# Loads of q, k and v from unit 6 on issued by GpSimd instead of SyncE, with all five engine orders solved anew

## The chip, the cores and the metric

The kernel runs on one core of a Trainium2 chip. A core has five engines that run side by side, each through its own list of instructions in order: TensorE (PE, matmuls; its weight loads are shown as PEld), VectorE (DVE), ScalarE (ACT), GpSimd (POOL) and SyncE (SP, which here only issues DMAs). They wait for one another by semaphores. DMAs are issued by SP, by POOL and in three places by ACT; the profile shows them as queues, q1 for those of SP, q0 for those of POOL and q10 for those of ACT. All queues share 16 DMA engines.

The metric is the time of one execution on the device in microseconds. Before the change it is 296.55 us, the median of three runs (296.13, 296.55 and 298.25).

## The reference

```python
def _attn_ref(q, k, v):                       # each (8, 8, 576, 64): batch, head, token, feature
    q_s = np.exp(q - np.max(q, axis=-1, keepdims=True))
    q_s = q_s / (np.sum(q_s, axis=-1, keepdims=True) + 1e-09)
    k_s = np.exp(k - np.max(k, axis=2, keepdims=True))
    k_s = k_s / (np.sum(k_s, axis=2, keepdims=True) + 1e-09)
    kv = np.einsum('bhsd,bhse->bhde', k_s, v)
    return np.einsum('bhsd,bhde->bhse', q_s, kv)

def _moe_ref(x, w_in, w_out):                 # x (4608, 512), w_in (512, 2048), w_out (2048, 512)
    h = x @ w_in
    g = np.where(h > 0.0, h, np.exp(np.minimum(h, 0.0)) - 1.0)
    return g @ w_out
```

The attention's output, with heads laid side by side, is the x of the second part. Everything is float32 at the boundary.

## The kernel before

**Attention in 16 units.** A batch's eight heads are cut into two units of four heads, so unit n is half of batch n // 2. For each unit q, k and v are loaded (`load`, L349; one DMA of 576 KB each) into the tiles `QR`, `KR` and `VR`. `QR` and `KR` exist twice and alternate by n % 2; `VR` exists once from unit 4 on (`raw`, L365, gives units 1 and 3 a second one). `stage1` (L385) takes exponentials of q and k on ACT (L392, L396), converts v to bfloat16 into `VB` (L276, on ACT or POOL), sums q's rows on DVE (L418), takes reciprocals (L420) and multiplies q by them into `QS` (L430, on POOL or DVE). From unit 4 on the transpose of `QS` is a DMA that SP issues (`turn`, L467) into the single tile `QT`, and `widen` copies it to float32 (`qsT`, L276, on ACT or POOL). `kv_mm` (L504) multiplies k by v on PE, two units in one go from unit 4 on; `m` normalizes the result (`MBLK`, L513 and L517); `ao_mm` (L535) makes the attention's output, and `xt` copies it into `XT`, a ring of 1,536 token columns.

**The feed-forward part in nine blocks.** Block j holds 512 tokens. `hg_mm` (L617) multiplies by w_in; ACT and DVE make g of it (L639, L641, L644; L648 and L650 in some groups of blocks 0 and 1). The product with w_out is plain for block 0 and half of block 1 (`out_mm`, L664), and from there on one level of Strassen's scheme on 256-column quarters (`pair`, L797). This needs differences of w_out's quarters once (`combos`, L724, into `TB` and `W2`) and sums of g's quarters for each half block (`add_sum`, L748, on POOL or DVE, into `SB` and `GR`). DVE adds the products into `OSB` tiles (L806), and `store` (L693) issues two DMAs for each tile. The four stores' tiles of block 0 are called `OSBX`. They lie where `TB` lies, so the third difference of each group (the one that writes the first third of `TB`) may not run before those stores have read their tiles. From block 1 on two `OSB` tiles alternate until the last three blocks, so a copy into one waits for the stores of the pair before.

**What sets the order.** The program records operations in a fixed numbering (0 to 1428) with their dependencies. The table `ORDER` (from L27) then gives for each engine the list of numbers in the order in which the engine runs them. An operation that may run on one of two engines (exponentials may not; conversions, copies, `QS` multiplications, differences and sums may) runs on the engine in whose list its number stands. So the order is written out, and no scheduler runs at build time. `emit` puts a semaphore wait ahead of an operation for each dependency that the engine does not know to be met; an engine that waits holds up everything behind it in its list. A load waits until its tile's former readers are done: q's for the multiplication into `QS`, k's for `kv_mm`, v's for the conversion into `VB`.

**Who issues what.** SP issues the loads of units 0 and 1 at the start, then the loads of units 6 to 15, all transposes and nearly all stores, in one list. POOL issues the loads of w_in (L374), of w_out (L382) and of units 2 to 5. The choice for units 4 to 15 is one line in `program`:

```python
                        self.load(n, t, due(n) - 20, "gp" if n < 6 else "sp")      # L944
```

Of the kernel before, what the change touches and what calls it, by code (L numbers as in the profile page):

```python
# [19 lines left out]
CASTS = 16  # L20
GROUPS, WHOLE = ((0, 4), (4, 6), (6, 8)), 6
NSP = 8
CAST0, CAST1 = "pair", "pair"
XT0, XT1, TP0, TP1 = "both", "both", ("act", "act"), ("act", "dve")
ISSUE = {"sp": 550, "act": 550, "gp": 740}
ORDER = {
    "pe": (  # L27
        "32 34 36 53 55 56 51 59 77 79 80 63 64 78 81 84 83 86 87 82 85 88 98 102 109 132 120 106 "
        "147 146 124 155 154 149 148 126 156 157 169 144 168 167 150 170 152 158 174 176 171 164 "
        "175 190 192 177 191 193 252 256 257 210 263 258 264 265 270 219 269 276 271 277 221 278 "  # L30
        "282 283 230 289 284 290 291 238 332 336 341 363 373 374 377 375 378 379 368 303 380 381 "
        "400 401 382 402 305 389 394 405 406 407 411 412 413 479 415 314 427 480 421 422 423 322 "
        "436 495 481 483 484 485 486 487 488 512 513 514 506 517 518 519 523 524 525 527 533 534 "
        "535 544 545 546 548 549 448 539 560 450 551 550 575 552 576 577 553 459 569 580 581 582 "
        "586 587 588 645 646 590 596 597 598 467 602 647 649 650 651 652 653 678 654 679 680 661 "
        "672 683 684 689 690 691 685 614 693 710 699 700 701 711 712 705 717 718 714 719 616 715 "
        "716 741 742 743 726 625 735 746 747 752 753 748 754 633 756 762 763 764 808 768 812 813 "
        "809 814 810 824 841 815 816 842 843 817 835 780 846 852 853 847 848 854 856 873 874 862 "
        "863 864 875 782 868 889 877 880 881 878 879 904 882 905 906 898 791 919 915 909 910 916 "
        "911 917 798 931 925 926 927 958 959 960 962 963 964 991 992 965 966 993 967 974 985 996 "  # L40
        "997 998 1002 1003 1004 1023 1024 1006 1025 1012 1013 1014 942 1018 1027 1028 1029 1030 "
        "1054 1031 1055 944 1032 1056 1039 952 1048 1059 1065 1066 954 1060 1067 1061 1069 1075 "
        "1088 1076 1089 1077 1153 1154 1081 1155 1092 1093 1094 1121 1090 1104 1160 1122 1123 1157 "
        "1158 1161 1095 1162 1159 1096 1097 1184 1115 1136 1126 1127 1132 1128 1133 1185 1134 1186 "
        "1148 1142 1143 1144 1169 1189 1190 1191 1195 1196 1197 1222 1178 1199 1218 1205 1206 1219 "
        "1223 1207 1283 1284 1211 1234 1220 1287 1224 1288 1285 1225 1251 1252 1226 1253 1227 1245 "
        "1266 1256 1257 1290 1291 1258 1262 1292 1263 1289 1264 1278 1272 1273 1274 1299 1314 1315 "
        "1316 1319 1349 1320 1308 1329 1321 1350 1325 1326 1327 1353 1365 1354 1366 1335 1336 1337 "
        "1351 1355 1382 1383 1356 1369 1357 1358 1367 1370 1384 1371 1398 1399 1387 1400 1372 1388 "
        "1393 1394 1389 1373 1374 1395 1409 1410 1411 1403 1404 1405 1417 1418 1419 1423 1424 1425 "),  # L50
    "act": (
        "24 28 40 44 21 23 3 33 39 37 58 52 54 65 66 113 89 92 93 95 99 100 103 110 111 133 121 108 "
        "134 115 114 136 138 137 151 153 178 197 165 172 184 181 223 194 198 206 248 249 253 259 "
        "260 266 220 296 235 272 273 279 231 232 285 286 292 293 239 307 333 337 338 317 302 364 "
        "365 369 370 441 316 390 391 395 396 306 319 416 417 428 429 323 452 437 438 496 497 462 "
        "507 508 528 529 607 540 547 541 561 451 618 562 465 570 571 464 461 591 592 628 468 648 "
        "603 604 773 662 663 673 674 627 694 695 713 784 706 707 617 630 740 727 728 626 736 737 "
        "757 758 769 770 811 779 825 826 936 840 836 837 781 857 858 796 794 869 876 870 890 891 "
        "946 793 899 903 900 792 920 921 932 961 933 975 976 986 987 1007 1008 1019 1020 1040 1041 "
        "1049 1050 955 1070 1071 1082 1083 1105 1091 1106 1120 1116 1117 1137 1138 1149 1150 1170 "  # L60
        "1171 1179 1180 1200 1201 1212 1213 1221 1235 1236 1250 1246 1247 1267 1268 1279 1280 1300 "
        "1301 1309 1310 1330 1331 1352 1381 1415 1422 1428 "),
    "dve": (
        "25 0 6 29 4 30 5 45 26 2 27 31 41 46 35 48 49 42 50 7 43 57 60 61 62 116 90 91 94 96 97 "
        "101 104 105 117 112 118 107 122 123 125 345 139 127 140 128 129 141 145 135 159 160 161 "
        "166 173 200 201 187 195 196 224 250 251 225 211 254 255 212 213 214 215 216 261 262 267 "
        "268 358 297 222 274 275 280 281 346 350 298 351 287 288 294 240 295 241 308 242 342 339 "
        "362 340 243 244 360 383 245 376 309 366 304 367 371 399 372 403 442 443 404 392 408 393 "
        "397 414 398 420 432 315 434 418 419 430 431 424 433 453 482 439 440 490 454 502 324 515 "
        "511 498 516 325 499 326 520 526 327 532 328 509 510 329 536 503 530 531 449 608 565 505 "  # L70
        "558 609 542 543 559 578 574 579 563 564 583 619 589 595 460 572 573 599 593 568 657 643 "
        "620 594 469 470 471 472 656 473 677 605 606 681 474 666 682 664 665 686 669 692 675 698 "
        "667 671 676 696 702 615 697 774 708 709 744 775 745 776 729 725 732 730 749 755 738 761 "
        "733 634 635 739 636 765 637 818 759 638 806 760 639 785 771 822 829 772 640 844 786 827 "
        "834 845 828 849 855 838 861 839 865 859 860 783 937 883 887 885 871 872 892 907 893 938 "
        "947 908 901 902 912 918 922 924 956 799 800 923 928 968 934 935 983 990 948 981 994 995 "
        "801 977 999 802 978 803 1005 988 804 1011 805 989 1033 1026 1015 1037 1009 1010 943 1021 "
        "945 1053 1022 1057 1034 1058 953 1042 1038 1043 1046 1062 1068 1074 1047 1051 1052 1098 "
        "1078 1072 1100 1073 1086 1156 1111 1109 1110 1087 1102 1163 1113 1084 1085 1107 1124 1108 "
        "1099 1125 1164 1103 1183 1118 1119 1129 1135 1141 1139 1140 1145 1187 1166 1188 1174 1151 "  # L80
        "1152 1192 1172 1198 1173 1204 1181 1182 1177 1208 1202 1230 1203 1216 1239 1214 1215 1237 "
        "1254 1286 1238 1243 1242 1229 1297 1255 1248 1259 1249 1269 1313 1265 1271 1270 1343 1294 "
        "1305 1281 1282 1302 1303 1317 1275 1307 1345 1318 1359 1311 1322 1328 1334 1332 1341 1333 "
        "1338 1312 1377 1363 1347 1362 1348 1360 1385 1368 1386 1401 1364 1402 1390 1397 1396 1416 "
        "1412 1413 1406 1420 1426 "),
    "gp": (
        "1 14 15 22 67 47 16 38 17 18 19 20 68 69 71 70 72 119 73 76 75 74 130 143 142 162 131 163 "
        "353 199 204 202 349 207 226 209 233 357 229 236 299 361 347 359 354 355 385 387 310 386 "
        "384 388 320 348 313 356 352 444 435 477 489 491 478 493 494 492 455 447 500 504 501 554 "
        "556 458 555 557 610 566 567 655 644 659 658 621 660 668 613 670 720 724 722 721 624 731 "  # L90
        "631 723 807 734 820 833 821 819 831 823 787 830 832 790 884 888 894 896 886 797 939 895 "
        "957 897 970 972 979 969 971 973 941 949 982 980 1035 984 951 1044 1045 1036 1114 1167 1168 "
        "1112 1165 1101 1176 1175 1228 1217 1241 1240 1232 1231 1233 1244 1295 1293 1304 1296 1306 "
        "1298 1361 1346 1344 1375 1342 1379 1376 1378 1380 "),
    "sp": (
        "8 9 10 11 12 13 203 205 208 218 227 234 217 228 186 182 188 179 185 237 183 189 180 300 "
        "301 247 334 335 344 343 318 246 311 410 321 409 312 425 426 445 446 463 522 456 521 457 "
        "331 330 537 538 466 584 611 585 612 600 601 629 475 476 623 622 687 688 704 703 777 632 "
        "750 641 778 767 766 751 642 851 850 788 789 795 866 867 913 914 930 929 940 1001 1000 950 "
        "1016 1017 1063 1064 1079 1080 1193 1130 1147 1210 1146 1209 1131 1194 1277 1276 1324 1260 "  # L100
        "1261 1340 1339 1323 1392 1391 1414 1407 1408 1421 1427 "),
}


# [169 lines left out]
class Gen:  # L274
# [578 lines left out]
    def program(self):  # L853
# [86 lines left out]
        def loads(*tn):  # L940
            def go():
                for t, n in tn:
                    if n < NU:
                        self.load(n, t, due(n) - 20, "gp" if n < 6 else "sp")  # L944
            return 0, go

        steps = [[first(2)], [wide(2), kv(2), loads(("q", 4), ("k", 4))],
# [133 lines left out]
```

## Time and profile before

| What | us |
|---|---|
| median of three runs | 296.55 |
| the profiled execution | 296.65 |
| its span, first to last instruction | 294.8 |
| outside the span | 1.85 |
| PE busy in the span | 279.6 |
| PE's first matmul of the feed-forward part starts at | 14.88 |
| last matmul ends at | 291.19 |
| POOL busy in the span | 174.0 |

The span is what the views below cover; the 1.85 us outside it stands in the execution's time alone. Times in a view count from the span's start. "POOL PS L797" or "DVE OSB L806" names an engine, the tile that is written and the line. A wait is named by the engine and line that waited and the one that released it. The timeline lists instructions with start, duration and what ended the idle time ahead of them; for SP, duration is the time to issue a DMA and not the transfer. The chain of waits is followed back from the last instruction to what released each step. Section 6 of the page gives the median time from the issue of a DMA to its landing. The granted TensorE clock is 1.00 throughout.

### The profile page before, as it was taken

To read this page: it belongs to the slowest core of one execution; us is meant where nothing else is said; L and a number is where in the kernel's file an instruction comes from. 1 tells how busy PE (TensorE), PEld (TensorE's weight loads), DVE (VectorE), ACT (ScalarE), POOL (GpSimd) and SP (SyncE) were. 2 spreads that over 40 slices of the span, in tenths; PEclk is the share of its full clock that TensorE was granted. 3 is DMA by queue.
4 is the path that set the end of the run, shared out by engine and by line. 5 is a ranking of instruction groups with operands and counts; after the bars stand their busy time and mean duration, and the time that the engine had idled before them with its cause. 6 is when DMAs were issued, how large, how long until landed. Compare 5 with 4: busy or idle time off the path is not lost.

```text
span 294.8 us, 5547 instructions
## 1 busy us (share of the span) xinstructions
PE 279.6 (95%) x2201; PEld 244.4 (83%) x2201; DVE 237.4 (81%) x446; ACT 204.4 (69%) x225; POOL 174.0 (59%) x169
## 2 busy tenths in 40 slices
PE   0899999999799999999999899999999999999995
PEld 0487878788698898989998789898989999998994
DVE  2858874988998899889899758877898976698983
ACT  5688848698799975998885679835574566665510
POOL 0870637773799898749580684979440603562651
PEclk9999999999999999999999999999999999999999
DMA  7999999899773487499419528043112002300325
GB/s 268 398 340 393 391 389 350 243 207 358 212 259 73 168 224 205 157 258 297 118 39 264 167 58 215 10 105 76 39 24 49 0 2 54 89 2 1 80 64 142
DMA packets 35946, 50.04 MB, mean 170 GB/s; under 512 B 16336, under 2 KB 17104, under 8 KB 35920
## 3 DMA queue, kind: packets, MB, share of 16 engines
q1 hardware_dynamic: 29680, 33.96, 40.4%
q0 software_dynamic: 6000, 15.47, 16.4%
q10 hardware_dynamic: 240, 0.26, 0.4%
q8 instruction: 17, 0.28, 0.4%
q14 instruction: 9, 0.07, 0.1%
HBM read 36.70 MB, written 9.44 MB: 156 GB/s over the span
## 4 chain that ended last, share of the span: by engine, by line
PE 81%; DMA 8%; POOL 3%; SPq 2%; issue 2%; ACT 1%; DVE 1%; POOLq 0%
PE PS L617 37%; PE PS L797 33%; PE PS L664 6%; DMA W<-in_moe_w_in_dram 3%; PE PS L535 2%; DMA KR<-in_k_dram 2%; DMA out_dram<-OSB 2%; DMA out_dram<-OSBX 2%; PE PS L504 1%; POOL QS L430 1%; SPq L693 1%; SPq L356 1%; POOL W L374 1%; POOL VB L276 1%; DVE TB L724 1%
## 5 line engine op out<-in xcount | busy, mean ns | idle before, releaser
L617 PE MATMUL PS<-XT,W 128*128 128x512 f32 x576 | 142.0, 393 | 0.4 <-DMA W<-in_moe_w_in_dram 0.4
L617 PEld LDWEIGHTS PS<-XT,W 128*128 128x128 f32 x576 | 105.2, 188 | 21.8 <-issue 0.8
L639 ACT ACTIVATE GE<-PS 128x1024 f32<-128x1024 f32 x72 | 73.5, 1024 | 54.3 <-PE PS L617 45.1
L644 DVE SCALAR_TENSOR_TENSOR GR<-PS,GE 128x512 fp32r<-128x512 f32 (+1 forms) x124 | 87.1, 704 | 23.4 <-ACT GE L641 21.9
L748 POOL TENSOR_TENSOR GR<-GR 128x256 fp32r<-128x256 f32 (+1 forms) x55 | 53.4, 984 | 38.1 <-DVE SB L748 29.1
L641 ACT ACTIVATE GE<-GE 128x1024 f32<-128x1024 f32 x64 | 67.9, 1061 | 1.8
L797 PE MATMUL PS<-W,GR 128*128 128x256 f32 x360 | 56.8, 283 | 1.7 <-ACT OSB L276 1.7
L797 PE MATMUL PS<-TB,GR 128*128 128x256 f32 x360 | 54.0, 283 | 0.0
L797 PEld LDWEIGHTS PS<-W,GR 128*128 128x128 f32 x360 | 50.5, 191 | 4.0 <-ACT OSB L276 2.2
L797 PEld LDWEIGHTS PS<-TB,GR 128*128 128x128 f32 x360 | 48.5, 191 | 0.8
L806 DVE TENSOR_TENSOR OSB<-OSB,PS 128x256 f32<-128x256 f32 x90 | 37.0, 413 | 9.4 <-PE PS L797 8.3
L430 POOL TENSOR_TENSOR QS<-QR,RZQ 128x1152 f16<-128x1152 f32 (+1 forms) x14 | 27.2, 1941 | 18.8 <-DVE RZQ L420 16.9
L748 POOL TENSOR_TENSOR SB<-GR 128x256 fp32r<-128x256 f32 (+1 forms) x20 | 19.9, 1000 | 22.0 <-DVE GR L644 21.3
L418 DVE TENSOR_REDUCE ZQ<-QR 128x18 f32<-128x1152 f32 (+2 forms) x18 | 21.8, 1209 | 9.3 <-ACT QR L416 5.4
L664 PE MATMUL PS<-W,GR 128*128 128x512 f32 x96 | 25.8, 398 | 1.7 <-DVE GR L644 1.7
L748 POOL TENSOR_TENSOR GR<-SB,GR 128x256 fp32r<-128x256 f32 (+1 forms) x23 | 21.9, 962 | 9.2 <-PE PS L797 7.4
L664 PEld LDWEIGHTS PS<-W,GR 128*128 128x128 f32 x96 | 17.4, 188 | 5.0 <-DVE GR L644 1.8
L748 DVE TENSOR_TENSOR GR<-GR 128x256 fp32r<-128x256 f32 (+1 forms) x35 | 20.2, 596 | 0.6 <-PE PS L797 0.5
L396 ACT ACTIVATE KR<-KR 128x1152 bf16<-128x1152 f32 x16 | 18.3, 1155 | 1.9 <-DMA KR<-in_k_dram 1.9
L276 POOL CAST qsT<-QT 128x1152 fp32r<-128x1152 f16 x10 | 11.5, 1149 | 10.7 <-PE PS L535 8.5
L797 PE MATMUL PS<-W,SB 128*128 128x256 f32 x112 | 17.3, 283 | 0.0
L392 ACT ACTIVATE QR<-QR 128x1152 f32<-128x1152 f32 x14 | 16.3, 1164 | 0.3 <-DMA QR<-in_q_dram 0.3
(57 smaller groups left out, 238.3 us busy)
## 6 DMA issues: line engine op xcount, KB each, us to landing
out_dram<-OSB SPq DMA_DIRECT2D x61, 128.0 KB, 2.4
QR<-in_q_dram SPq DMA_DIRECT2D x12, 576.0 KB, 4.6
KR<-in_k_dram SPq DMA_DIRECT2D x12, 576.0 KB, 6.3
VR<-in_v_dram SPq DMA_DIRECT2D x12, 576.0 KB, 5.0
W<-in_moe_w_out_dram POOLq DMA_DIRECT2D x4, 1024.0 KB, 12.2
QR<-in_q_dram POOLq DMA_DIRECT2D x4, 576.0 KB, 10.6
VR<-in_v_dram POOLq DMA_DIRECT2D x4, 576.0 KB, 11.3
KR<-in_k_dram POOLq DMA_DIRECT2D x4, 576.0 KB, 9.7
```

Of the source, the lines that this page charges most:

```text
L392: S.add("act", t_act(1152, False), lambda e: e.activation(flat(q), flat(q), AF.Exp), key - 3, X=[f"qR{i}0", f"qR{i}1"])
L396: S.add("act", t_act(1152, False), lambda e: e.activation(ek[:, :, :, :].rearrange("p h c d -> p (h c d)"), flat(k), AF.Exp), key - 2, X=[ ...
L418: S.add("dve", t_dve(m), lambda e, qp=qp, zp=zp: e.tensor_reduce(zp, qp, AX.X, ALU.add), key - 3, R=[f"qR{i}{x}" for x in xs], W=[f"ZQ{i}{ ...
L430: lambda e, qp=q[:, :, a:b, :], rz=rz, dst=qs[:, :, a:b, :]: e.tensor_tensor(dst, qp, rz, ALU.mult),
L617: last = e.matmul(P[:, t * 512:(t + 1) * 512], self.W1[:, kc, tt * 128:(tt + 1) * 128], self.XT[:, kc, rc:rc + BLK], start=(kc == 0), stop ...
L639: S.add("act", t_act(1024, True), lambda e: e.activation(ge, P, AF.Exp), key, W=gw + over, X=banks)
L641: S.add("act", t_act(1024, False), lambda e: e.activation(ge, ge, AF.Relu, bias=1.0, scale=-1.0), key, X=gw)
L644: S.add("dve", t_dve(512 if j else 1024), lambda e, u=u: e.scalar_tensor_tensor(*(x[:, :, u, :] if j else x for x in (gt, P)), 0.0, ge[:, ...
L664: last = e.matmul(dst, self.tile(jb, jj, ts), self.W2[:, jj, c0:c1], start=(jj == 0), stop=(jj == 15))
L748: lambda e: e.tensor_tensor(dst, a, b, op), key, R=R, W=W, X=X, after=after)
L797: last = e.matmul(dst, a[i][:, y_, :], b[i][:, y_, :], start=start and i == 0 and y_ == 0, stop=stop and i == len(grps) - 1 and y_ == z - ...
L806: S.add("dve", t_dve(256), lambda e: e.tensor_tensor(dst, a, b, ALU.add), key, R=R, W=W, X=X, after=after)
```

## The change

The loads of units 6 to 15 (ten units, three each, 30 DMAs) are issued from POOL's list; SP's list keeps the first six loads, the transposes and the stores. All five lists are new, and with them the engine of 177 operations, 30 of them the loads. The lines that differ, with the long tables cut:

```diff
+SPLIT_RINGS = True
 ORDER = {
...
     "gp": (
-        "1 14 15 22 67 47 16 38 17 18 19 20 68 69 71 70 72 119 73 76 75 74 130 143 142 162 131 163 "
-        "353 199 204 202 349 207 226 209 233 357 229 236 299 361 347 359 354 355 385 387 310 386 "
...
+        "1 27 15 14 67 16 38 17 18 19 20 119 68 69 72 71 70 73 76 75 74 130 115 138 143 162 131 163 "
+        "345 353 204 205 207 208 349 217 218 226 233 234 228 357 346 236 237 246 351 247 359 361 "
...
     "sp": (
-        "8 9 10 11 12 13 203 205 208 218 227 234 217 228 186 182 188 179 185 237 183 189 180 300 "
-        "301 247 334 335 344 343 318 246 311 410 321 409 312 425 426 445 446 463 522 456 521 457 "
...
+        "8 9 10 11 12 13 203 186 189 227 180 182 185 183 179 188 335 334 300 344 343 311 409 425 "
+        "426 410 445 522 521 456 537 538 585 584 600 601 611 687 688 622 703 704 750 751 777 767 "
...
 }
...
-                        self.load(n, t, due(n) - 20, "gp" if n < 6 else "sp")
+                        self.load(n, t, due(n) - 20, "gp")
```

`SPLIT_RINGS` is read nowhere. In these lists 203, 227, 300, 311 and so on are transposes; 179 to 189 are the stores of block 0; 750 and 751 are the two stores of one tile of block 3; 204, 208 and 234 are the loads of v of units 5, 6 and 7, and 207, 233 and 236 their conversions; 205 is the load of q of unit 6; 226 is the multiplication into `QS` of unit 5; 346, 347 and 351 are differences of w_out's quarters.

Of the operations that change engine besides the loads, 47 go from DVE to POOL and 47 from POOL to DVE (sums, differences and multiplications into `QS`), 10 from POOL to ACT and 4 from ACT to POOL (conversions of v, `widen`), 17 from ACT to DVE and 22 from DVE to ACT (copies out of PSUM). On PE the same products are computed in another order, with 12 warm-up matmuls where there were 13.

## The prediction

> **What bounds the kernel now.** First the engines' busy times, section 1 of the page:
>
> ```profile
> PE 279.6 (95%) x2201; PEld 244.4 (83%) x2201; DVE 237.4 (81%) x446; ACT 204.4 (69%) x225; POOL 174.0 (59%) x169
> ```
>
> PE is the bound. So the next view is what PE waited for from 23 us on, when all weights for the first blocks are there (columns: us in total, times, longest):
>
> ```profile
> PE PS L797 <- ACT OSB L276: 1.7, 2, 1.2
> PE PS L664 <- DVE GR L644: 1.7, 1, 1.7
> PE PS L617 <- DMA W<-in_moe_w_in_dram: 0.4, 1, 0.4
> ```
>
> That is all of it in 272 us. The timeline puts the gaps at 74.29 (1.68 us), 165.91 (1.17) and 170.92 (0.55), and 0.42 at 22.96. What no change of order can take away is PE's own work; what can be won after 23 us is 1.68 + 1.17 + 0.55 = 3.40 us. The w_in gap is set by bytes: DMA runs at nine tenths or more in the slices around it.
>
> The chain of waits (start, us, what) shows what is behind the first gap and the second:
>
> ```profile
> 67.52 5.05 DMA out_dram<-OSBX
> 72.57 1.02 issue
> 73.60 1.72 DVE TB L724
> 75.31 0.61 DVE GR L644
> ...
> 75.97 1.20 PE PS L664 x4
> ...
> 161.49 5.14 DMA out_dram<-OSB
> ...
> 166.65 0.38 ACT OSB L276
> ```
>
> Both are stores that land about 5 us after their issue. DVE stood 1.02 us ahead of a difference into `TB` until a store of block 0 had read its tile, and PE waited for the L644 behind it; ACT waited 2.32 us for an `OSB` tile, and the copies it does for PE came late twice. Section 6 has a store's usual price:
>
> ```profile
> out_dram<-OSB SPq DMA_DIRECT2D x61, 128.0 KB, 2.4
> ```
>
> SP's timeline says why the late one took 5.14:
>
> ```profile
> 157.14 0.59 SPq L356 DMA_DIRECT2D KR<-in_k_dram  x1
> 157.78 0.47 SPq L356 DMA_DIRECT2D QR<-in_q_dram  x1
> 160.33 1.75 SPq L693 DMA_DIRECT2D out_dram<-OSB  x3
> ```
>
> Loads of 576 KB went out just ahead of the stores on the same queue. The first case is the same: SP issued v, k and q loads at 62.27, 63.73 and 64.24 and then the stores of block 0.
>
> **The change part by part.** *Stores.* Without loads in SP's list, the stores of block 0 stand around the transpose of unit 5 with nothing else, and 750 and 751 are next to one another, where before 751 stood behind 767 and 766, which waited for DVE until 160.31. At 2.4 us each (section 6) 751, issued at about 157.7, lands near 160, five us before ACT asked for the tile (164.33, where its L641 ended). For block 0, 227 will be issued at about 62 (next part), its issue takes 1.3 to 1.5 us, and six stores at 0.60 us end at 67.4 and land by 70, where before the last landed near 76. DVE reached its difference at 72.6. Both stalls go: -3.40 us. Next late behind the first is then ACT's L639 and L641 of block 1's last group, which end at about 73.6 by their rows (1.03 and 1.06 us after that group's matmuls); L644 ends at 74.3, and PE asks at 74.2 to 74.9.
>
> *A store on a queue of its own.* That the loads no longer delay it is not shown by a row here: at 8.5 us POOL's first w_in load was issued beside SP's loads and landed at 13.69, just after SP's last one (12.71), as if behind it. From that row the stores would win nothing; from the 2.4 us of stores that stand behind no load, all. I take the second, since few loads are then in flight at once (DMA share 0.68 from 57 to 172 us). The Trainium skill, "DMA: Bandwidth & Descriptors", has a section for each: "Queues, rings and completion order" says each DMA engine goes round the queue rows packet by packet, so a store would pass a load; "Issuing engines are not separate DMA queues" says spreading DMAs over engines saves only issue time. By the first the 3.40 us are won, by the second they stay.
>
> *Loads on POOL.* A load on POOL occupies it, and lands later than on SP:
>
> ```profile
> 48.98 0.73 POOL L356 DMA_DIRECT2D VR<-in_v_dram  x1 [0.30 <-POOL VB L276]
> 50.30 2.12 POOL L430 TENSOR_TENSOR QS<-QR,RZQ 128x1152 f16<-128x1152 f32 x1 [0.58 <-DVE RZQ L420]
> 52.38 1.74 POOL L724 TENSOR_TENSOR TB<-W 128x512 fp32r<-128x512 f32 x1
> 54.26 1.15 POOL L276 CAST VB<-VR 128x1152 bf16<-128x1152 f32 x1
> ```
>
> This one landed 5.2 us after its issue (SP's loads with an empty queue: 3.8 to 4.1). Thirty at 0.74 us are 22.2 us of POOL. Off POOL come six conversions net at 1.15 (-6.9); the swap of 47 for 47 with DVE is +1.9 by the rows (0.84 and 1.33 for sums of 256 and 512 columns, 2.12 for `QS`, 1.3 and 2.4 for differences). POOL: 174.0 + 22.2 - 5.0 = 191 us, 65% of the span: no bound as a whole. ACT gets 6.9 us and some copies (204 to about 213), DVE loses two or three. Each load also waits in POOL's list for its tile's readers, and all sums behind it wait too.
>
> *Where this bites first.* In POOL's new list the load of v of unit 5 (204), the load of q of unit 6 (205) and the conversion of that v (207) follow one another; the multiplication of 2.12 us and the difference of 1.74 that lay between are elsewhere. 204 goes out at about 49.8: ahead of it POOL now makes a difference of 2.4 us, and ACT the conversion of unit 4 (49.7). It lands at 55.0, the conversion ends at 56.2, and PE's `kv_mm` of units 4 and 5, which had its turn at 55.78 with 0.37 us to spare, starts at 56.4 to 56.5: +0.7. Behind 207 stand 208, 349 (1.5), 217, 218 and the `QS` of unit 5 (226), which ends near 62.1 instead of 59.80, so its transpose is issued at 62.2 instead of 60.93; `widen` (now on ACT) and `ao_mm` of unit 5, which PE asks for at 68.8, have about 0.5 us left. The w_out loads wait for `QS` of unit 2 (119) and go out near 23.4 instead of 16.70. The last w_in load lands at 25.91 and the first of w_out at 28.62 before; now that one lands about 0.4 us later, and PE asks at 31.09: nothing.
>
> *The start.* POOL's first w_in load stands behind a multiplication, as before behind k's landing (8.2): both near 8.5. The matmuls of the feed-forward part begin at about 16.0 instead of 14.88, but all attention work of units 0 and 1 is then behind, and group 4's weights land near 23.24 either way: 0, with 0.5 either side.
>
> *POOL's dense stretch.* From 57.3 to 171.7 us (columns PE, PEld, DVE, ACT, POOL):
>
> ```profile
> 57.30:171.70 114.40, 111.00 (x918) 98.00 (x918) 100.83 (x189) 93.28 (x100) 81.88 (x71) 1.00 0.68 199
> ```
>
> Counting both lists between the `QS` of unit 5 and that of unit 13 by the same rows gives 78.8 us before and 95.1 after, 24 loads among it: 16.3 more, 98.2 of 114.4 (0.86). POOL's idle time falls from 32.5 to 16.2 us. If its waits shrink that far, it costs nothing; if only to two thirds, 21.7, PE is 5.5 us late. The nearest row is DVE, busy 100.83 (0.88) in the same stretch, which made PE wait for nothing but that store; so I take a quarter, 1.4 us.
>
> *Elsewhere.* PE's products, the last 15 us and the stores at the end have the same work; the lists there differ in single places. I take 0.
>
> Sum: 296.65 - 3.40 + 0.7 + 1.4 = 295.35, against a median of 296.55 (the profiled execution is 0.1 above it).
>
> **The rivals.** *Nothing new comes:* both costs hidden, 296.65 - 3.40 = 293.25. For it: PE lost nothing to POOL in all of 23 to 291 us. Against: the kv_mm above has only 0.37 us of cover. 0.14.
>
> *POOL becomes the bound of 57 to 172 us.* In one list the loads wait for the readers on ACT, DVE and PE, and the sums behind them, which PE's L797 needs within a few tenths (one sum ended at 106.14, its product began at 106.75), wait too. It decides when POOL's waits there stay above 16.2 us. At two thirds of before: 296.65 - 3.40 + 0.7 + 5.5 = 299.45; at three quarters (24.4) 302.2. For it: 0.86 in order is near DVE's 0.88, and POOL's L748 waits for DVE, 29.1 us for its sums and 21.3 for L644 in the span. Against: most of these were waits for work not yet due. 0.33.
>
> A rule bears on this rival. A load issue of POOL at 31.98 beside DVE's L648 took 1.01 us, others 0.70 to 0.79, so 0.3 is the most that the trace shows; L648 ends at 58 us. The Trainium skill, "SBUF — State Buffer", section "SBUF: two separate sides", warns that DVE's two-port operations lock POOL out while it writes descriptors, 620 ns growing to 3,100. By it each load beside such an operation would cost POOL 2.5 us.
>
> *The queues do not part:* the stores wait all the same, 296.65 + 0.7 + 1.4 = 298.75. 0.08.
>
> **How the numbers follow.** Forecast 0.45, nothing new 0.14, POOL the bound 0.33, queues not parted 0.08. One per cent of 296.55, about what a measurement of this kernel tells from no change, is 293.6 and 299.5. Faster is the first rival, 0.14; slower is POOL the bound, 0.33; the rest 0.53. The range goes from 293.0 (nothing new, with half of the start's 0.5) to 301.5, which leaves out the worst part of POOL the bound. I predict 295.4.
>
> **What would show it.** In the profile after: no PE wait on L644 at 74 us, stores of `OSBX` that land in 2 to 4 us instead of 6.2, no ACT wait for an `OSB` landing; a PE wait of about 0.7 at L504 near 56; POOL near 191 us, 30 issues of 0.74. PE waits on POOL's L748 of over 5 us in all would make POOL the bound; stores that still take 5 us, the last rival. Issues on POOL well over 0.8 us, or a w_in wait of over 1 us, would break the sum.

## The result, and the profile after

The changed kernel takes 314.6 us (median of four executions, 313.33 to 317.45) against 297.4 us for the kernel before on the same chip: 1.059 times, with a 95% interval of 1.050 to 1.068. It is slower, 13.1 us above the top of the range. The profiled execution took 314.52 us, with a span of 312.7 us and a mean granted TensorE clock of 0.982, where before had 1.000. The ratios in this document are taken over executions in the chip's faster state alone, so some differ a little from the quotient of the medians. Line numbers after are one higher than before (L748 is L749).

Section 1 of the page, busy time, share of the span and instructions of each engine:

```profile
PE 286.8 (92%) x2200; PEld 247.1 (79%) x2200; DVE 251.1 (80%) x441; ACT 211.4 (68%) x236; POOL 186.3 (60%) x193
```

POOL, which got thirty more instructions, is still the least busy, at 186.3 us (191 were expected of it). DVE is 13.7 us busier, with five operations fewer. PE's waits (engine and line that waited, what released it: us in total, times, longest):

```profile
PE PS L798 <- DVE OSB L277: 4.6, 1, 4.6
PE PS L798 <- DVE GR L749: 3.3, 1, 3.3
PE PS L536 <- DVE MBLK L518: 1.8, 1, 1.8
PE PS L798 <- ACT OSB L277: 1.7, 2, 1.2
...
PE PS L505 <- POOL VB L277: 0.9, 1, 0.9
```

Only the last names POOL. From 23 us on PE's gaps are 15.85 us in all, in twelve places (0.75 of it a wait for w_in), where before had 3.40 in three. The chain of waits shows what lay behind the three largest (start, us, what):

```profile
52.11 10.96 DMA QT<-QS
63.09 1.17 ACT qsT L277
...
89.86 5.64 DVE GR L749 x2
95.50 0.35 DVE OSB L277
95.89 3.78 PE PS L798 x16
...
150.88 5.10 DVE SB L749
```

The transposes of unit 4 took 10.96 us, where before they took 3.1. Twice a sum of g's quarters on DVE, 128x256, took over five microseconds; when nothing is beside it, it takes 0.41. The timelines of POOL and DVE at the second of the three (start, us, operation):

```profile
88.97 0.73 POOL L357 DMA_DIRECT2D VR<-in_v_dram  x1
89.70 0.72 POOL L357 DMA_DIRECT2D QR<-in_q_dram  x1
90.44 2.13 POOL L431 TENSOR_TENSOR QS<-QR,RZQ 128x1152 f16<-128x1152 f32 x1
...
93.74 1.14 POOL L277 CAST VB<-VR 128x1152 bf16<-128x1152 f32 x1
...
89.78 5.72 DVE L749 TENSOR_TENSOR GR<-SB,GR 128x256 fp32r<-128x256 f32 x2
```

The row of DVE holds two sums; the first took 5.39 us of it. DVE asked at 89.78, while POOL issued its second load, and was done at 95.16. POOL's row ends at 94.88, and up to there it has no pause. At 150.8 us it is the same: a load, three operations without a pause that end at 155.68, and a DVE sum from 150.79 to 155.97. Two of the three gaps are then paid a second time. These are stretches of 2 us behind the gap at 91 us (columns: PE, PEld, DVE, ACT, POOL, granted clock, DMA share, GB/s):

```profile
94.00:96.00 2.00, 0.11 (x1) 0.12 (x1) 2.00 (x4) 0.00 (x0) 0.88 (x1) 0.50 0.86 173
96.00:98.00 2.00, 2.00 (x10) 2.00 (x11) 1.94 (x5) 0.00 (x0) 0.00 (x0) 0.50 0.00 0
98.00:100.00 2.00, 2.00 (x10) 1.90 (x10) 0.57 (x2) 1.15 (x2) 1.42 (x2) 0.50 0.00 0
```

The clock is at half in all three, and the 3.78 us in the chain are sixteen matmuls that take 1.9 at the full clock. The same happened at 69.3 to 72.7 us, behind the gap of 1.84 us at 65.4. Behind the third gap, 3.27 us at 153.1, the clock stayed full.

### The profile page after: what moved, and what is told of

The parts are those of the page before. It is cut to its first block, busy times and chain, and to the rows that moved or that the text cites. A ratio compares the mean times of both kernels' runs of the same rounds, so it can differ in the third digit from the quotient of the medians.

```text
span 312.7 us, 5525 instructions
## 1 busy us (share of the span) xinstructions
PE 286.8 (92%) x2200; PEld 247.1 (79%) x2200; DVE 251.1 (80%) x441; ACT 211.4 (68%) x236; POOL 186.3 (60%) x193
## 4 chain that ended last, share of the span: by engine, by line
PE 56%; DMA 16%; DVE 16%; ACT 7%; POOL 2%; issue 1%; SPq 1%; DVEq 0%
PE PS L618 28%; PE PS L798 24%; DMA VR<-in_v_dram 7%; DVE GR L645 5%; DVE GR L749 5%; DMA QT<-QS 4%; DMA out_dram<-OSB 3%; DMA QR<-in_q_dram 2%; ACT GE L640 2%; DVE SB L749 2%; PE PS L536 2%; ACT GE L642 2%; DVE OSB L807 2%; PE PS L505 1%; ACT QR L393 1%
## 5 line engine op out<-in xcount | busy, mean ns | idle before, releaser
L618 PE MATMUL PS<-XT,W 128*128 128x512 f32 x576 | 144.5, 397 | 2.4 <-DVE GR L645 1.6
L645 DVE SCALAR_TENSOR_TENSOR GR<-PS,GE 128x512 fp32r<-128x512 f32 (+1 forms) x124 | 87.3, 705 | 22.4 <-ACT GE L642 20.3
L642 ACT ACTIVATE GE<-GE 128x1024 f32<-128x1024 f32 x64 | 67.8, 1060 | 1.6
L749 POOL TENSOR_TENSOR GR<-GR 128x256 fp32r<-128x256 f32 (+1 forms) x51 | 48.7, 971 | 26.7 <-PE PS L798 16.5
L798 PE MATMUL PS<-TB,GR 128*128 128x256 f32 x360 | 56.2, 286 | 0.0
L798 PEld LDWEIGHTS PS<-TB,GR 128*128 128x128 f32 x360 | 50.1, 194 | 1.1
L749 POOL TENSOR_TENSOR SB<-GR 128x256 fp32r<-128x256 f32 (+1 forms) x23 | 22.0, 959 | 37.1 <-DVE GR L645 20.5
L431 POOL TENSOR_TENSOR QS<-QR,RZQ 128x1152 f16<-128x1152 f32 (+2 forms) x12 | 23.9, 1989 | 13.2 <-DVE RZQ L421 11.9
L749 DVE TENSOR_TENSOR GR<-GR 128x256 fp32r<-128x256 f32 (+1 forms) x39 | 29.6, 766 | 1.5 <-PE PS L798 0.8
L749 POOL TENSOR_TENSOR GR<-SB,GR 128x256 fp32r<-128x256 f32 (+1 forms) x26 | 25.5, 991 | 7.6 <-DVE GR L749 4.9
L277 ACT ACTIVATE OSB<-PS 128x256 f32<-128x256 f32 (+1 forms) x23 | 9.0, 396 | 23.3 <-PE PS L798 16.3
L277 POOL CAST VB<-VR 128x1152 bf16<-128x1152 f32 (+1 forms) x10 | 11.0, 1102 | 13.9 <-DMA VR<-in_v_dram 13.9
## 6 DMA issues: line engine op xcount, KB each, us to landing
W<-in_moe_w_in_dram POOLq DMA_DIRECT2D x2, 1024.0 KB, 10.1
```

The costliest lines, as they stand in the source:

```text
L277: return e.activation(dst, src, AF.Copy) if e is self.nc.scalar else e.tensor_copy(dst, src)
L431: lambda e, qp=q[:, :, a:b, :], rz=rz, dst=qs[:, :, a:b, :]: e.tensor_tensor(dst, qp, rz, ALU.mult),
L618: last = e.matmul(P[:, t * 512:(t + 1) * 512], self.W1[:, kc, tt * 128:(tt + 1) * 128], self.XT[:, kc, rc:rc + BLK], start=(kc == 0), stop ...
L642: S.add("act", t_act(1024, False), lambda e: e.activation(ge, ge, AF.Relu, bias=1.0, scale=-1.0), key, X=gw)
L645: S.add("dve", t_dve(512 if j else 1024), lambda e, u=u: e.scalar_tensor_tensor(*(x[:, :, u, :] if j else x for x in (gt, P)), 0.0, ge[:, ...
L749: lambda e: e.tensor_tensor(dst, a, b, op), key, R=R, W=W, X=X, after=after)
```

## The experiments

All times, each against the kernel before on the same chip:

| kernel | median, us | ratio to before, 95% interval |
|---|---|---|
| the change | 314.6 | 1.059 (1.050 to 1.068) |
| its lists, loads on SP (`a_loads_on_sp`) | 303.3 | 1.024 (1.018 to 1.031) |
| its lists, loads on ACT (`a_loads_on_act`) | 304.9 | 1.029 (1.021 to 1.037) |
| before's lists, loads on POOL (`b_loads_on_pool`) | 308.1 | 1.041 (1.035 to 1.047) |
| one load later (`a_205`) | 312.0 | 1.045 (1.037 to 1.052) |
| five loads moved (`a_rows`) | 313.9 | 1.054 (1.047 to 1.062) |
| seven loads on SP (`a_seven_on_sp`) | 308.3 | 1.036 (1.032 to 1.041) |
| ten loads on SP (`a_ten_on_sp`) | 303.5 | 1.017 (1.006 to 1.027) |
| before's lists, one load of thirty on SP (`b_pool_one_back`) | 306.9 | 1.033 (1.028 to 1.037) |
| two (`b_pool_two_back`) | 306.4 | 1.027 (1.020 to 1.035) |
| four (`b_pool_four_back`) | 303.1 | 1.019 (1.015 to 1.023) |
| changed lists on SP, one swap (`a_sp_one_swap`) | 304.2 | 1.020 (1.015 to 1.026) |
| changed lists on SP, one copy earlier (`a_sp_copy_first`) | 303.6 | 1.020 (1.013 to 1.026) |
| before, three stores earlier (`b_stores`) | 294.4 | 0.992 (0.988 to 0.995) |
| before, five stores earlier (`b_stores_two`) | 295.2 | 0.991 (0.987 to 0.995) |

**The two halves of the change.** The diff has two parts, the engine that issues the loads and the new lists. One kernel has the lists alone, one the loads alone, and a third lets ACT issue them:

```diff
# a_loads_on_sp: the changed kernel; the 30 loads at the times at which POOL issued them
-                        self.load(n, t, due(n) - 20, "gp")
+                        self.load(n, t, due(n) - 20, "gp" if n < 6 else "sp")
# b_loads_on_pool: the kernel before; the 30 loads at the times at which SP issued them
-                        self.load(n, t, due(n) - 20, "gp" if n < 6 else "sp")
+                        self.load(n, t, due(n) - 20, "gp")
# a_loads_on_act: as a_loads_on_sp
+                        self.load(n, t, due(n) - 20, "gp" if n < 6 else "act")
```

> The changed kernel with all its lists, except that the 30 loads of units 6 to 15 stand in SP's list again, at the places where the changed kernel's trace has their issue times. Theory 'port and rings': most of the 18 us goes away, 296 to 302 us, no DVE sum over 2.5 us, transposes land in 3 to 5 us. Rival 'orders': the new lists cost it, 308 to 316 us whoever issues the loads.

> The kernel before with all its lists, except that the 30 loads of units 6 to 15 stand in POOL's list, at the places where its trace has their issue times. Theory 'port and rings': 303 to 318 us, with DVE sums of 2 to 6 us that begin within 1 us of a load's issue, and transposes of 5 to 11 us. Rival 'orders': 295 to 300 us, as POOL has over 30 us to spare between 57 and 172 us.

> The changed kernel with all its lists, except that the 30 loads are issued from ACT's list, again at their issue times. They are then neither on POOL nor in the queue of the stores and transposes. Theory 'port and rings': DVE's sums are back at 0.4 to 1.3 us, transposes beside loads still take 5 to 11 us: 299 to 308 us. Rival 'orders': 308 to 318 us, with ACT 16 us fuller.

Loads on POOL cost 308.1 - 296.2 = 11.9 us with the old lists (before was 296.2 on that chip). With the new ones they cost 314.6 - 303.3 = 11.3, or 17.2 - 7.1 = 10.1 when each kernel is compared with before on its own chip. The new lists cost 303.3 - 296.2 = 7.1 us without any load on POOL. So both halves are slower, and measured apart they come near the whole: 11.9 + 7.1 = 19.0 for 17.2. The 303.3 us lie between the two expectations, as neither had a price for the lists alone; 308.1 and 304.9 lie where the first theory had them, though in `b_loads_on_pool` the transposes of units 4 and 5 landed after 3.0 and 4.3 us and not 5 to 11. From ACT the same loads cost 1.6 us, although ACT is 68% busy in the changed kernel: it is POOL that is dear, not an issue as such.

**The suspected operations alone.** Two small programs time a DVE addition of 128x256 beside rows of POOL additions of 128x512, and transposes and stores beside loads. Both leave out the reference's work.

> This kernel does none of the reference's work. It sets up short blocks, each started by one ACT copy. Ten blocks have a row of five POOL instructions (additions of 128x512, 1.3 us each, or conversions of 128x1152, 1.15 us), with or without loads of 576 KB issued by POOL among them, and beside them one DVE addition of 128x256 with two inputs in SBUF (0.41 us when alone); in one block that addition reads one input from PSUM. Ten blocks time a DMA transpose (six) or two stores (four) on SP beside no load or one to three loads of POOL's, ACT's or SP's queue. All twice. Theory 'port and rings': (1) without a load ahead DVE waits for at most about one POOL instruction, so its addition takes 0.4 to 1.8 us; with a load issued just ahead of the row it waits for several, 3 to 7 us, and with one input in PSUM 0.4 to 0.5; (2) a transpose lands 2.9 us after issue when alone, 6 to 12 us beside two POOL loads or two ACT loads, since each of its small packets takes turns with a large one, and 5 to 7 us behind two loads on its own queue; stores beside two POOL loads land in 2.4 to 4 us, behind two SP loads in 5 to 6. Rival 'orders': a load makes no difference to DVE, which waits as long beside any dense row of POOL's, and a transpose takes 3 to 4 us beside loads of another queue.

> Leaves out all of the reference's work; it times one VectorE addition of 128x256 with two operands in SBUF beside rows of GpSimd additions of 128x512 (about 1.26 us each). Known from the first measurement: 0.41 us alone, 0.98 to 1.47 us beside a row without a load, 6.1 to 7.0 us when a load stands ahead of a row of five. Theory 'the load makes GpSimd keep VectorE out until GpSimd stops': load and ten additions 12 to 13 us; a stop of GpSimd in the row (a wait for ScalarE that is not yet met) ends it there, so 2 to 4 us; a load, then the stop, then the row: 1 to 1.5 us; a load issued by ScalarE: 1 to 1.5 us. Rival 'a fixed time after a load' (its descriptors are written for some us): ten additions are no longer than five, 6 to 7 us, and a request made two microseconds later waits two microseconds less. Open on both: whether a wait that is already met ends it, and whether a copy of one SBUF operand is kept out as well.

The timeline of the second, in three of its blocks: a load and ten additions, a load with a pause behind its first addition, and a load from ACT:

```profile
21.80 0.72 POOL L260 DMA_DIRECT2D QR<-in_q_dram  x1 [1.34 <-ACT GO L233]
...
22.55 12.22 POOL L285 TENSOR_TENSOR SB<-GR 128x512 fp32r<-128x512 f32 x10
22.86 12.19 DVE L264 TENSOR_TENSOR DV<-GR 128x256 fp32r<-128x256 f32 x1
...
54.45 1.28 POOL L285 TENSOR_TENSOR SB<-GR 128x512 fp32r<-128x512 f32 x1
54.77 1.25 DVE L264 TENSOR_TENSOR DV<-GR 128x256 fp32r<-128x256 f32 x1
58.77 1.26 POOL L285 TENSOR_TENSOR SB<-GR 128x512 fp32r<-128x512 f32 x1 [3.05 <-ACT GO L280]
...
76.78 6.32 POOL L285 TENSOR_TENSOR SB<-GR 128x512 fp32r<-128x512 f32 x5 [0.74 <-ACT GO L233]
78.07 1.48 DVE L264 TENSOR_TENSOR DV<-GR 128x256 fp32r<-128x256 f32 x1
```

In these blocks the addition waits for the whole row, 12.19 us, if POOL issued a load ahead of it, and gets in after one operation if POOL pauses there. Behind a row without a load it took 0.98 to 1.48 us, so at most the rest of the operation that was running. Five additions behind a load made it 6.1 to 7.0. Waits in the row that are already met do not help (6.09); a pause between the load and the row does (0.48). With one operand in PSUM it took 0.41 behind a load; a copy from SBUF to SBUF was held like the addition (5.96). An addition that was asked for 2 us later took 3.92, again to the end of the row. So the rival, a fixed time after a load, falls: the hold lasts as long as the row does. The Trainium skill, "SBUF — State Buffer", section "SBUF: two separate sides", says that DVE and POOL share a pair of ports, and that whoever starts first has it for the whole instruction. The rows without a load agree (at most 1.48 us). Behind a load the measurement goes beyond that: ten instructions, not one. One block has a second load behind the first addition, and there DVE got in at the end of that load's issue, after 1.88 us, both times.

The transposes' time from issue to landing was 3.3 us alone, 3.9 beside one load of POOL, 5.0 to 5.9 beside two and 7.0 to 7.8 beside three. Stores took 2.3 us alone, 4.1 to 4.4 beside two loads of POOL, and 4.7 to 5.0 behind two loads on SP's own queue. Beside two loads of ACT a transpose took 4.3 and stores 3.3 to 3.5. So loads on POOL's queue rather than SP's took about half a microsecond off a store, and did not bring it down to the 2.4 us that the prediction took. The expectation missed these sizes: transposes beside two loads of POOL or ACT were to take 6 to 12 us, and stores beside two of POOL 2.4 to 4.

**Moving loads in POOL's list.** Two kernels test the two mechanisms in place:

```diff
# a_205: the q load of unit 6 behind 207, the conversion of unit 5's v
-        "345 353 204 205 207 208 349 217 218 226 233 234 228 357 346 236 237 246 351 247 359 361 "
+        "345 353 204 207 205 208 349 217 218 226 233 234 228 357 346 236 237 246 351 247 359 361 "
# a_rows: 318 and 301 behind 352, 629 behind 621, 795 behind 823, 789 behind 894
-        "354 360 383 318 301 310 352 320 386 388 432 313 348 312 321 434 444 489 435 477 446 491 "
+        "354 360 383 310 352 318 301 320 386 388 432 313 348 312 321 434 444 489 435 477 446 491 "
...
```

> The changed kernel with one load moved in GpSimd's list: the q load of unit 6 is issued behind the conversion of unit 5's v rather than ahead of it, so that it no longer runs beside the transposes of unit 4. Theory 'transposes pay for loads beside them': these transposes land 4 to 6 us after their issue instead of 11.0, ScalarE's widening no longer waits 5.2 us, the 1.84-us gap of TensorE near 65 us goes and with it the half clock of 69 to 73 us; 310 to 312 us, 3 to 4.4 us less than the changed kernel. Rival 'the transposes are hidden, all is VectorE held out behind loads': 314 to 315 us, since no load ahead of a held addition is moved.

> The changed kernel with five loads moved in GpSimd's list, none in time by more than some microseconds: the two ahead of the row at 90 us go behind its first two operations, the one at 150.5 us behind the 2.1-us product of that row, the two at 183.6 and 200 us behind the additions that followed them. Theory 'VectorE's additions are held out behind a load': the additions of 5.4 and 5.2 us take 0.4 to 2.5, TensorE's gaps of 4.65 and 3.27 us shrink below 1.5 each, the half clock of 94 to 100 us goes; 305 to 309 us. Rival 'a dense GpSimd holds VectorE out with or without a load': the additions stay above 4 us, 313 to 316 us.

In `a_205` the transposes of unit 4 landed 5.4 us after their issue, for 11.0, and ACT waited for them no longer: that part of the collision is shown, and the median of 312.0 us is at the edge of the first theory's range. But PE lost as much at that place as before (a gap of 2.18 us at 62.3, then half the clock): with two loads now ahead of a row, DVE's scaling L649 was held from 59.48 to 63.11. This trace also shows what the theory doesn't explain. The two loads and the row of 89 us are unchanged, and DVE asked at the same point of them:

```profile
88.24 0.73 POOL L357 DMA_DIRECT2D VR<-in_v_dram  x1
88.97 0.72 POOL L357 DMA_DIRECT2D QR<-in_q_dram  x1
89.04 0.76 DVE L749 TENSOR_TENSOR GR<-SB,GR 128x256 fp32r<-128x256 f32 x2
89.71 2.14 POOL L431 TENSOR_TENSOR QS<-QR,RZQ 128x1152 f16<-128x1152 f32 x1
```

Asked for 0.07 us after the second issue began, both sums ran free. In the changed kernel it was 0.08 us after, and the first was held for 5.39. So the order of the lists alone doesn't decide whether an operation is held. The trace is of the shortest of four executions (308.4 us; the others took 311.1 to 314.0), and whether the others were held there isn't shown. In `a_rows` no DVE sum was held over 2.4 us, as expected, and PE ended the seventh group of block 2 at 102.2 us, for 107.9 in the changed kernel. It gave this back by 180 us: the v load of unit 13, now behind an operation of 2.1 us, held ACT up for 3.39 us, waits of ACT for a store (1.45) and a q load (3.56) followed, and PE's gaps at 154 and 163 us with the half clock behind them cost it 7.8 us against the lists without loads on POOL. The time of 313.9 lies where the rival put it, while the held operations went as the theory said; so a move in the list was no clean test.

**Taking loads away from POOL instead.**

```diff
# a_seven_on_sp: the changed kernel; loads 205, 318, 301, 612, 629, 795, 789 in SP's list
-                        self.load(n, t, due(n) - 20, "gp")
+                        self.load(n, t, due(n) - 20, "sp" if (n, t) in ((6, "q"), (9, "v"), (8, "q"), (12, "q"), (13, "v"), (15, "v"), (15, "q")) else "gp")
# a_ten_on_sp: 208, 217 and 218 as well: (6, "v"), (6, "k"), (7, "k")
```

> The changed kernel with seven of the thirty loads back on SyncE, each put into SyncE's list at the time at which GpSimd issued it: the six that stood ahead of a held addition (units 9 v, 8 q, 12 q, 13 v, 15 v and 15 q) and the q load of unit 6, that ran beside the transposes of unit 4. Twenty-three stay on GpSimd. Theory 'a load ahead of a row without a pause holds VectorE out': most of the 11 us that all thirty cost on this list goes, 303 to 307 us. Rival 'each load on GpSimd costs its share, for its issue, wherever it stands': 7 of 30 of 11.3 us, so 2.6 us, 311 to 313 us.

> The changed kernel with ten of its thirty loads on SyncE: the seven of the run above (308.3 us) and the three of units 6 v, 6 k and 7 k, which stood ahead of the row at 58 to 65 us in that run, beside a VectorE scaling of 6.53 us (1.24 when it runs free) and the only TensorE gap of it that the lists with all loads on SyncE do not have. Twenty loads stay on GpSimd. Theory 'the held operations are the whole price': as with all loads on SyncE, 302.5 to 304.5 us. Rival 'each load costs something beside them': 20 of 30 of 11.3 us above that, 310 to 311 us; 307 to 309 us if only three more loads' share goes.

Seven gave 6.3 us, between the two expectations (308.3 us). The trace shows the rest in one place. DVE's timeline:

```profile
58.99 6.53 DVE L649 TENSOR_SCALAR GE<-GE 128x1024 f32<-128x1024 f32 x1
```

A load of v stood ahead of that row; PE had a gap of 5.08 us behind it and 6.8 us of half clock, 3.7 of them with PE at work again. By the sixth group of block 1 the kernel was 6.5 us later than with all loads on SP (74.3 for 67.8), and at its end 5.2: nothing was added after that place. With three more loads away the scaling took 0.80 us and the kernel 303.5: what all thirty on SP give (303.3), with twenty still on POOL. The rival's 310 to 311 is excluded. On these lists the price is not per load: nine loads ahead of rows without a pause and one beside the transposes cost all of it. Ten others were not moved for comparison.

**The same on the lists of before.**

```diff
# b_loads_on_pool, with loads back at their old places in SP's list
-                        self.load(n, t, due(n) - 20, "gp")
+                        self.load(n, t, due(n) - 20, "sp" if (n, t) == (9, "q") else "gp")                     # one
+                        self.load(n, t, due(n) - 20, "sp" if (n, t) in ((9, "q"), (10, "v")) else "gp")         # two
+                        self.load(n, t, due(n) - 20, "sp" if (n, t) in ((9, "q"), (10, "v"), (9, "v"), (8, "k")) else "gp")  # four
```

> The kernel before with its loads on GpSimd (308.1 us in the run above), and one of the thirty, the q load of unit 9, back on SyncE at its old place: it stood on GpSimd between two table sums with a product behind them, while a VectorE addition took 3.96 us near 97 us, and TensorE's clock was halved from 103 to 108 us behind it. Theory 'held out behind a load': the addition takes 1 to 2 us, the half clock goes, 302 to 304.5 us. Rival 'its share of the issues': 0.4 us of 11.9, 307 to 309 us.

> The kernel before with its loads on GpSimd but for two on SyncE at their old places: the q load of unit 9 as in the run above (306.9 us), where the addition still took 5.39 us, and the v load of unit 10, which stood ahead of the same row, so that taking the other away had only left that row without a pause. Twenty-eight stay on GpSimd. Theory 'held out from the last load ahead of the row to GpSimd's next pause': the addition takes at most 2.5 us, TensorE's 2.26-us gap at 102 us and the half clock behind it go, 301 to 303.5 us. Rival 'a dense row holds VectorE with or without a load': the addition stays above 4 us, 306 to 308 us.

> The kernel before with its loads on GpSimd but for four on SyncE at their old places: the two of the run above (306.4 us) and those of units 9 v and 8 k, which GpSimd issued at 84.6 us, at the start of a stretch of 16 us without a pause. Twenty-six stay on GpSimd. Theory 'held out from any load until GpSimd pauses, however long that is': the addition near 97 us takes 0.7 to 2.5 us instead of 4.54, TensorE's 2.07-us gap behind it and the half clock go, 301 to 303 us. Rival 'a dense stretch of this length does it alone': the addition stays above 4 us, 306 to 307 us.

One and two loads gave 1.2 and 1.7 us by the medians (2.4 and 2.0 when each kernel is compared with before on its own chip). That is about what the rivals had, and the addition was still held, for 5.39 and 4.54 us. I had looked for a load too near to the request. POOL's timeline in the run with two back:

```profile
84.62 0.73 POOL L356 DMA_DIRECT2D VR<-in_v_dram  x1
85.35 0.72 POOL L356 DMA_DIRECT2D KR<-in_k_dram  x1
...
99.27 2.11 POOL L430 TENSOR_TENSOR QS<-QR,RZQ 128x1152 f16<-128x1152 f32 x1
```

and DVE's there, then DVE's in the run with four back:

```profile
97.39 4.54 DVE L748 TENSOR_TENSOR SB<-GR 128x512 fp32r<-128x512 f32 x1
```

```profile
96.19 1.17 DVE L748 TENSOR_TENSOR SB<-GR 128x512 fp32r<-128x512 f32 x1
```

The two loads were issued 11 us before the request, and POOL did not pause from 84.6 to 101.4 us. With them gone POOL runs the same operations without a pause up to 102 us, and the sum takes 1.17 us. So the dense row alone does not do it, and a load 11 us away still did. The time, 303.1, is just above what was expected; 26 loads on POOL then still cost about 5.6 us (303.1 against 297.5 for before on that chip), part of it in gaps of 1.53 and 1.56 us at 122 and 172 us. These were not taken apart.

**The 7 us of the new lists.**

```diff
# a_sp_one_swap: a_loads_on_sp; in DVE's list the difference 355 behind the sums 385 and 387
-355 385 387
+385 387 355
# a_sp_copy_first: a_loads_on_sp; in DVE's list the copy 376 ahead of them
-385 387 376
+376 385 387
```

> The changed kernel's lists with the loads back on SyncE (303.3 us in the run above), and in VectorE's list one table sum moved behind the two additions that follow it, so that these are asked for before GpSimd's 2.4-us product begins rather than beside it. It asks what the new lists cost without any load on GpSimd. Theory 'a good part of their 7 us is VectorE held out by GpSimd's long products, as they happen to lie': the additions of 2.35 and 1.49 us take 0.4 to 1.0, TensorE's gap of 2.68 us at 88 us shrinks below 1, 300.5 to 302 us. Rival 'the price lies at the start and in many small waits': 303 to 304 us.

> The changed kernel's lists with the loads back on SyncE (303.3 us), and in VectorE's list one copy out of PSUM moved ahead of two additions: TensorE's gap of 2.68 us at 88 us ends with this copy, which stands behind additions that GpSimd's long product and table sum keep waiting (2.35 and 1.49 us for 0.41). No load stands there. Theory 'the lists put VectorE's additions beside GpSimd's long operations, and TensorE behind them': the gap goes, 300.5 to 302 us. Rival 'TensorE then waits for the additions themselves, some matmuls later': 302.5 to 304 us.

Both times are near the rivals'. The swap did not do what it was meant to: the second sum was still beside POOL's long product (2.34 us), and the gap stayed 2.68 us, so it tests little. The copy took that gap away, and three of 0.69, 0.89 and 0.91 us came within five microseconds. So no single wait carries the 7 us. In the trace of the lists without loads on POOL, PE's gaps from 23 us on are 7.75 us in ten places instead of 3.40 in three, and its products take 283.0 us for 279.6, spread over all lines. DVE's sums of g and differences of w_out's quarters also took 16.4 us longer in all than at their free durations (0.41, 0.68 and 1.21 us by their width), for 7.1 before, though POOL issued none of the thirty loads there. That they cause the 7 us is not shown, and why the lists came out so stays open.

**A version that beats both.** The stalls of before are stores behind loads on one queue; SP idled ahead of them.

```diff
# b_stores: the kernel before, SP's list: stores 186 and 185 ahead of 227, store 751 next to 750
-        "8 9 10 11 12 13 203 205 208 218 227 234 217 228 186 182 188 179 185 237 183 189 180 300 "
+        "8 9 10 11 12 13 203 205 208 218 186 185 227 234 217 228 182 188 179 237 183 189 180 300 "
-        "750 641 778 767 766 751 642 851 850 788 789 795 866 867 913 914 930 929 940 1001 1000 950 "
+        "750 751 641 778 767 766 642 851 850 788 789 795 866 867 913 914 930 929 940 1001 1000 950 "
# b_stores_two: besides, 334 and 335 ahead of the loads 301 and 247
```

> The kernel before with its loads where they were, on SyncE, and three stores moved up in SyncE's list: the two stores of the third output tile (units 5's side) go ahead of the transposes of unit 5, into a stretch where SyncE idles, and the second store of a pair near 157 us directly behind the first. Theory 'the stalls of before are stores queued behind loads, and can be had without moving a load': TensorE's gaps of 1.68 us at 74.3 and 1.17 us at 165.9 go, 293.0 to 295.0 us. Rival 'those transposes or loads are then late': the gap comes back at another line, 296 to 298 us.

> The kernel before with the three stores moved up as in the run above (294.4 us), and two more, the stores of the next output tile near 79 us, ahead of the q load of unit 8 and the k load of unit 9 in SyncE's list: in the run above VectorE's copy into that tile waited for them and TensorE lost 2.41 us at 84.6 us. Theory 'a store behind loads is late by what they take': that gap goes, 292 to 293.5 us. Rival 'the next store is late in its place': 294 to 295 us.

`b_stores` is 0.8% faster than before, and its trace has none of the three gaps of before past 23 us. A new one of 2.41 us at 84.6 had the same cause one tile later, and is gone in `b_stores_two`, which yet gains nothing more (295.2 us, just above its rival's 294 to 295): 1.28 us at 91.6 came in its place. The gain of the change's aim, 3.4 us by the trace, is to be had at 2.3 to 2.8 without moving a load.

## Why the prediction was wrong

**POOL's dense stretch, +1.4 us: the step that failed.** It let a fuller POOL cost time only where PE or another engine waits for POOL's results, and took "a quarter" of what such waits could be. PE's waits name POOL once, 0.9 us. What came was the other direction: POOL in a row behind a load keeps DVE's SBUF operations out, and PE waits for DVE. All loads together, with unit 4's transposes among the causes, made 10.1 to 11.3 us where the sum had 1.4: gaps of 15.85 us for the 7.75 of the same lists on SP, and 3.8 us of slower matmuls at half the clock. The trace of before could not show the hold as such, but it had the sign: the difference into `TB` of 1.72 us in the chain takes 0.68 when it runs free, and stood beside a product of POOL, without a load. The rule on ports that the prediction took from the Trainium skill ("SBUF — State Buffer", section "SBUF: two separate sides") was read for POOL's wait alone, 0.3 us; its other half, DVE waiting, was the one to price, though it speaks of one instruction at a time.

**Rival "POOL becomes the bound".** Right in its sign, wrong in its mechanism and its size (299.45 to 302.2): POOL's waits were not what ran short.

**The stores, -3.40 us.** Half right. No wait on L645 at 74 us is left beyond 0.2 us. But the stores of `OSBX` landed after 5.3 to 9.0 us, not 2 to 4, and ACT still waited 7.1 us for an `OSB` tile, in two places; behind one of them PE lost 1.17 us at 161.6, as much as at 165.9 before. I chose the round-robin rule over "Issuing engines are not separate DMA queues" of the Trainium skill's "DMA: Bandwidth & Descriptors". The stores measured alone, 4.1 to 4.4 us beside POOL's loads against 4.7 to 5.0 behind SP's, stand near the second. The rival "the queues do not part" was so the better half of the story, at a price that the rest buried.

**Transposes, not priced.** The step gave `widen` and `ao_mm` of unit 5 half a microsecond of slack and left the time of the transposes at 3.1. Unit 4's took 11.0; with the new lists and all loads on SP it was 5.7.

**kv_mm of units 4 and 5, +0.7 us.** Right: a gap of 0.90 us at 57.26, released by POOL's `VB`. It stays at 0.76 with 205 on SP, so it comes from where 204 and 207 stand.

**The start, 0, and elsewhere, 0.** With the new lists and all loads on SP, PE is 1.8 us late at 54.9 us and 6.7 at the end; this is the 7.1 us above, which the sum put at nothing. The prediction took lists of equal work for equal time and checked single places.

**What would show it.** Of the signs named, 30 issues of 0.72 to 0.78 us, POOL near 191 us and no PE wait on POOL's L749 pointed to the forecast; all three came true while the time was missed by 19 us. No sign watched DVE's own durations.

## What to carry to other kernels

An operation that is moved to an engine is priced by whom that engine shares something with, not only by its own free time: here loads on the least busy engine cost 10 to 12 us, and in the new lists twenty of thirty cost nothing. In a kernel like this one keep loads off GpSimd where a row of its operations without a pause follows and VectorE works from SBUF to SBUF; let SyncE issue them, with due stores put ahead of loads. And after an edit look for the next wait before the gain is counted: four of these kernels lost one gap and found another within some ten microseconds.

## What the runs showed of the hardware

- Behind a load issued by POOL, DVE could be held until POOL paused: 12.19 us for 0.41 in the small program, and in the kernel an addition asked for 11 us after the load, which took 4.54. A pause of 0.30 us was enough at 137 us in the changed kernel. Held were sums with both operands in SBUF, a copy and the scaling L649; a row sum of `QR` (L418, 1.34 us) ran as ever in such a row. Some got in earlier, within 2 us of a load's issue (3.96 us in `b_loads_on_pool`, 3.62 in `a_205`, 2.09 in the changed kernel, 1.88 in the small program). Others did not: at 134.7 us in the changed kernel a second load came after the request, and the sum waited 2.77 us for POOL's pause. Two sums that the changed kernel and `a_205` asked for at the same point of the same row were held in one and free in the other. What decides is not known from these runs.
- The granted clock fell to half behind some gaps of PE and not behind others. It fell behind 1.84 us in the changed kernel (3.9 us after the gap began), and not behind 3.27 us there, while in `a_205` the same 3.27 us were followed by half clock. It fell behind 2.68 us in `a_loads_on_act`, and not behind the same 2.68 us in `a_loads_on_sp`. Within the kernels each stretch of half clock lasted 3.41 or 6.83 us. What decides between them was not tried.
- Each further load of 576 KB in flight from POOL added 0.6 to 2 us to a transpose that SP's queue carries, in the small program; in the kernel one load less took unit 4's from 10.96 to 5.42 us (`a_205`).
